# A new order at the start of a fused kernel: twelve units on half the tokens first, attention steps between products

## The chip, the cores and the metric

The kernel runs on one core of a Trainium2 chip. A core has a matrix engine (PE in the rows, with its weight loads on PEld), a vector engine (DVE), a scalar engine (ACT), a general-purpose engine (POOL) and a queue engine (SP) that here only starts DMAs. Each engine works through its own list in order, and engines wait for one another by semaphores. The metric is the device time of one execution in microseconds, as the median of several runs.

## The reference, cut to what matters

Inputs are a decaying linear attention over 4 sequences of 768 tokens (8 heads of 48), a dense mixture of four experts, and a two-layer network:

```python
# attention: state S (complex, 48x48 per head) decays by a_re + i a_im, magnitude capped at 0.999
S = a_t * S + outer(k_t, v_t);  y_t = q_t @ real(S)
# mixture, x is 3072 x 384, four experts with 1024 hidden columns each
p = probs / (probs.sum(-1) + 1e-9)
out += p[:, e] * (relu(x @ w1[e]) @ w2[e])
# second network, 2048 hidden columns
h = out @ w_in;  result = maximum(0.01 * h, h) @ w_out
```

## The kernel before, in words

**Tiling.** The 3072 tokens are 24 chunks of 128 (attention) and 6 groups of 512 (the two networks); a group is four chunks. The hidden columns are cut into units of 128: 32 for the experts, 16 for the second network. Per group and unit, `gemm_in` does nine matmuls into a PSUM tile `ph` (each product of fp32 numbers is split into three fp32r products: high x high, high x low, low x high), DVE makes `hp` from it, ACT its high part `hh`, DVE its low part `hl`, and `gemm_out` does nine matmuls into three accumulators. The loop over `order` at the end issues `gemm_in(s + 2)` ahead of `gemm_out(s)`, so a unit has two positions of time for `hp`, `hh` and `hl`.

**Attention.** A chunk has two generators. `elementwise(c)` has 18 steps on DVE, ACT and POOL and ends in `ft`, which `by_head` reorders by six small DMAs into `hd`. `products(c)` does the matmuls: transposes `pt` (copied to `kt`), scores `sc` (masked to `att`), `pm` (the state update `st`), `py`, and transposes `px`, of which `xh` and `xl` are the input of the units.

**Weights.** A unit's raw weights (384 KB) come by DMA into one of four `raw` tiles, are split into a high and a low part `wt` (768 KB, one of seven tiles, `WTS`) by ACT (L408) and POOL (L409), and are stored to the scratch `ws`; the later five groups load them from there. For the first units, `cast_early` (letter `s`) and `rest_early` (letter `m`: two fp32 matmuls, L429 and L430, and an ACT copy) make the low part on the matrix engine.

**What sets the order.** Nothing is scheduled by a tool: engines run what the code issues, in the order of issue. Before the first unit the string `PLAN` sets it, a letter a step: `0` to `3` a step of `elementwise` of that chunk, `p` and `q` of `products(0)` and `(1)`, `s` and `m` as above, `n` the probabilities. Then the loop over `order` runs, and its `tick` (two per position, at most three steps each) takes steps from `background`: the rest of chunks 2 and 3, their products (`r`, `t`), then the chunks of the later groups, by the table `pace`. In the loop `split_unit(s + 4, 0)` and `split_unit(s + 3, 1)` are issued ahead of the ticks and of `split_h(s + 2)`, so on ACT a weight cast stands ahead of the `kt` copies and the `hh` of its position. `load_unit(s + 7)` is issued at the top of a position.

**The start.** The first 8 units (`NHALF`) of group 0 run on 256 tokens (chunks 0 and 1) while chunks 2 and 3 are still to come, then the same 8 units on the other 256 tokens, with their weights loaded again from `ws`, and then units 8 to 31 on 512 tokens. A "half block" below is nine matmuls of 256 columns, the `gemm_in` or the `gemm_out` of a unit on 256 tokens.

Of the kernel before, what the change touches and what calls it, by code (L numbers as in the profile page):

```python
# [10 lines left out]
F32 = mybir.dt.float32  # L11
# [20 lines left out]
WU = 2 * DM  # L32
AR_MIN = 0.76
NHALF = 8
PLAN = (
    "0101001010101011" "01ss0000mm" "00sss11mm000" "1111ppsm23111qq"
    "23232n3pp23p2ppqq3q23qqpq23m"
)
MAXT = 3
KN = 3.0  # L40
PT = 32
TPOOL = 6
MARGIN = 2.0
LAG = 2
E2 = 20
RAWS = 4
WTS = 7
DEC = 33.0
# [1 line left out]
ESTEPS = 17  # L50
LOADSTEP = 9
NSTEPS = ESTEPS + len(PSTEPS)
WAIT = 4
AR_MAX = 1e4
AI_MAX = 1.0
PI = 3.1415925
# [5 lines left out]
def fused_kernel(  # L62
# [13 lines left out]
    V, A, G, SP, PE = nc.vector, nc.scalar, nc.gpsimd, nc.sync, nc.tensor  # L76
# [6 lines left out]
    with ExitStack() as fast:  # L83
# [58 lines left out]
        def load_chunk(c, part=None):  # L142
            if part in (None, 0):
                pool = p_el2 if c in (1, 3) else p_in
                t = pool.tile([P, 4, NG, P], F32, name="aaqk", bufs=2)
                vt = pool.tile([P, DM], F32, name="vt", bufs=2 if c in (1, 3) else 3)
                inputs[c] = (t, vt)
            t, vt = inputs[c]
            if part is None:
                SP.dma_start(t, attn[c])  # L150
            else:
                SP.dma_start(t[:, 2 * part : 2 * part + 2], attn[c][:, 2 * part : 2 * part + 2])
            if part in (None, 1):
                SP.dma_start(vt, v[c])
# [3 lines left out]
        def table(name):  # L158
            if tables[0] != name:
                A.preload_act_table_set(name)  # L160
                tables[0] = name

        def elementwise(c):
            t, vt = inputs[c]
# [78 lines left out]
        def by_head(c):  # L243

            ft, vt = feats[c]
            pool = p_el2 if c in (1, 3) else p_el
            hd = pool.tile([2 * D, H, 2 * P + 1], F32, name="hd")
            for ri in range(2):
                for i in range(NG):
                    row = ri * D + i * DG  # L250
                    (A if c < 2 and (i == ri or i == 2 - ri) else SP).dma_start(hd[row : row + DG], ft[:, ri, i])
            feats[c] = (ft, hd, vt)


# [3 lines left out]
        def products(c):  # L258
# [7 lines left out]
            for ri in range(2):  # L266
                pt = ps_a.tile([P, NG, P], F32, name="pt", tag="pa")
                for i in range(NG):
                    PE.transpose(pt[:, i], ft[:, ri, i, P : 2 * P], ident)  # L269
                A.copy(  # L270
                    kt[:, :, ri * D : (ri + 1) * D].rearrange("t h (r d) -> t r d h", d=DG),
                    pt.rearrange("t r (d h) -> t r d h", h=H),
                )
                yield
# [25 lines left out]
            for h in range(H):  # L300
                PE.matmul(py[:, h], att[:, h], vt[:, h * D : (h + 1) * D], start=True, stop=first)  # L301
                if not first:
                    PE.matmul(py[:, h], hd[:, h, :P], old[:, h], start=False, stop=True)  # L303
                if h == 3:
                    yield
            y = pool.tile([P, DM], F32, name="y", bufs=1)
# [59 lines left out]
        whole, halves = (0, TG), ((0, TG // 2), (TG // 2, TG))  # L366
        first_stage = lambda g: [(g, u, whole) for u in range(NU1)]
        second_stage = lambda g: [(g, u, whole) for u in range(NU1, NU)]
        order = [(0, u, half) for half in halves for u in range(NHALF)] + first_stage(0)[NHALF:]
        begins = [0]  # L370
        for g in range(1, NGRP):
            begins.append(len(order) - NHALF)
# [6 lines left out]


        raws, wts, pbs, hs, x2 = {}, {}, {}, {}, {}
        seen = set()
        fresh = [u not in seen and not seen.add(u) and u < NU1 for _, u, _ in order]

        def load_unit(s):

# [7 lines left out]
        def load_split(s):  # L394
            if s >= len(order):
                return
            u = order[s][1]
            if not fresh[s]:
                wts[s] = p_w.tile([P, 2, 2, DM], F32R, name="wt", bufs=WTS)
                SP.dma_start(wts[s].bitcast(F32), ws[u])  # L400

# [34 lines left out]
        def load_pb(s):  # L436
            if s >= len(order) or order[s][1] >= NU1 or order[s][1] % 8 or order[s][2][0]:
                return
            g, e = order[s][0], order[s][1] // 8
            pb = p_h.tile([P, TG], F32, name="pb", bufs=2)  # L440
            SP.dma_start(pb, pn_d[e : e + 1, g * TG : (g + 1) * TG].to_broadcast([P, TG]))
            pbs[g, e] = pb

# [32 lines left out]
        def gemm_out(s, acc):  # L476
            u, (t0, t1) = order[s][1:]
            first, last = u in (0, NU1) and t0 == 0, u in ends
            wt = wts.pop(s)[:, 1]
            hh, hl = hs.pop(s)  # L480
            for dc in range(NG):
                cols = slice(dc * P, (dc + 1) * P)
                out = acc[dc][:, t0:t1]
                PE.matmul(out, wt[:, 0, cols], hh, start=first, stop=False)  # L484
                PE.matmul(out, wt[:, 1, cols], hh, start=False, stop=False)  # L485
                PE.matmul(out, wt[:, 0, cols], hl, start=False, stop=last)  # L486


        def zipped(*gens):
            gens = list(gens)  # L490
            while gens:
                for x in list(gens):
                    if next(x, gens) is gens:
                        gens.remove(x)
                yield

        def run_all(*gens):
            gens = list(gens)
            while gens:
                gens = [x for x in gens if next(x, gens) is not gens]  # L500

        with tc.manual_schedule():
            table("natural_log_exp_and_others")
# [9 lines left out]
                load_unit(s)  # L513
            steps = {str(c): elementwise(c) for c in range(CPG)}
            steps.update(zip("pqrt", (products(c) for c in range(CPG))))
            early_halves = iter([(s, part) for s in range(6) for part in (0, 1)][: PLAN.count("s")])
            for x in PLAN + "m" * 8:
# [9 lines left out]
            for s in (5, 6):  # L527
                load_unit(s)
            split_unit(3, 0)

            def background():
                for _ in range(2):
                    next(steps["2"])
                    yield
                for _ in zipped(steps["2"], steps["3"]):
                    yield
                load_chunk(4)
                for _ in range(WAIT):
                    yield
                for x in "rt":  # L540
                    yield from steps[x]
# [29 lines left out]

            dec = decoding()

            first = 2 + max(0, ESTEPS + 1 - min(PLAN.count("2"), PLAN.count("3"))) + WAIT + E2 - PLAN.count("r") - PLAN.count("t")
# [34 lines left out]
            for s in range(len(order)):  # L609
# [12 lines left out]
                if u not in ends:  # L622
                    tick(now)
                split_h(s + 2, hp)
                if fresh[s]:
                    SP.dma_start(ws[u], wts[s].bitcast(F32))
                gemm_out(s, acc)
                now += step
# [214 lines left out]
```

## Time and profile before

| | |
|---|---|
| median of 3 runs | 1481.2 us (1477.52 to 1483.52) |
| profiled execution | 1478.36 us, span 1476.6 us |
| PE busy | 1402.4 us, 95% of the span |
| DVE, ACT, POOL busy | 59%, 38%, 18% |
| mean granted clock of PE | 0.976 |
| first unit's first matmul | 66.74 us |
| first half block on tokens 256 to 511 | 123.46 us |
| group 0's accumulators read out | 285.67 us |

The span is the time from the first to the last instruction of the profiled execution; 1.76 us of that execution lie around it. PE is busy nearly all the time from 170 us on, so what stands between a shorter time and this one is either matmul work or the idle and slow stretches of the first 170 us. A granted clock of 1.00 is 2.4 GHz, 0.50 is 1.2 GHz. A row of the time line gives start, duration, engine, line, operation and tile, with the idle time before it and what ended it in brackets; an fp32 matmul shows as two records, and a record's duration overlaps the next one's start.

### The profile page before, as it was taken

To read this page: it belongs to the slowest core of one execution; us is meant where nothing else is said; L and a number is where in the kernel's file an instruction comes from. 1 tells how busy PE (TensorE), PEld (TensorE's weight loads), DVE (VectorE), ACT (ScalarE), POOL (GpSimd) and SP (SyncE) were. 2 spreads that over 40 slices of the span, in tenths; PEclk is the share of its full clock that TensorE was granted. 3 is DMA by queue.
4 is the path that set the end of the run, shared out by engine and by line. 5 is a ranking of instruction groups with operands and counts; after the bars stand their busy time and mean duration, and the time that the engine had idled before them with its cause. 6 is when DMAs were issued, how large, how long until landed. Compare 5 with 4: busy or idle time off the path is not lost.

```text
span 1476.6 us, 18540 instructions
## 1 busy us (share of the span) xinstructions
PE 1402.4 (95%) x6978; PEld 1177.2 (80%) x6978; DVE 864.7 (59%) x1504; ACT 564.8 (38%) x961; POOL 264.5 (18%) x244
## 2 busy tenths in 40 slices
PE   3858999999999999999999999999999999999997
PEld 1858888888777888788888888888888888888886
DVE  7556887788988898785454554554443333333332
ACT  5424565444345434455234354233332111323232
POOL 2120565412223223221011110110110000100000
PEclk9569999999999999999999999999999999999999
DMA  7288789986788789588567477576465665556561
GB/s 192 43 207 301 212 255 298 331 291 208 273 301 290 250 305 319 153 303 245 153 234 222 151 242 216 188 222 199 154 199 172 231 207 196 190 188 208 190 212 65
DMA packets 91043, 325.49 MB, mean 220 GB/s; under 512 B 10464, under 2 KB 32064, under 8 KB 90944
## 3 DMA queue, kind: packets, MB, share of 16 engines
q1 hardware_dynamic: 87488, 318.71, 67.1%
q10 hardware_dynamic: 3456, 5.51, 1.3%
q8 instruction: 56, 0.92, 0.3%
q14 instruction: 43, 0.35, 0.1%
HBM read 262.72 MB, written 42.52 MB: 207 GB/s over the span
## 4 chain that ended last, share of the span: by engine, by line
PE 58%; DVE 2%; ACT 0%; issue 0%; DVEq 0%; ACTq 0%
PE ph L455 27%; PE acc L484 9%; PE acc L486 9%; PE acc L485 9%; PE sc L280 1%; PE py L301 1%; PE py L303 1%; PE pm L289 1%; PE pt L269 0%; DVE hl L473 0%; DVE hp L460 0%; PE px L311 0%; DVE d L349 0%; ACT hh L472 0%; DVE d L355 0%
## 5 line engine op out<-in xcount | busy, mean ns | idle before, releaser
L455 PE MATMUL ph<-xh,wt 128*128 128x512 f32 (+1 forms) x1200 | 397.9, 388 | 0.0
L484 PE MATMUL acc<-hh,wt 128*128 128x512 f32 (+1 forms) x888 | 350.8, 395 | 5.2 <-ACT o L604 5.1
L486 PE MATMUL acc<-hl,wt 128*128 128x512 f32 (+1 forms) x888 | 342.9, 386 | 4.5 <-DVE hl L473 4.5
L485 PE MATMUL acc<-hh,wt 128*128 128x512 f32 (+1 forms) x888 | 341.5, 385 | 0.0
L472 ACT CAST hh<-hp 128x512 fp32r<-128x512 f32 (+1 forms) x296 | 180.4, 610 | 418.2 <-DVE hp L460 326.5
L473 DVE TENSOR_TENSOR hl<-hp,hh 128x512 fp32r<-128x512 f32 (+1 forms) x296 | 213.4, 721 | 150.3 <-ACT hh L472 149.1
L455 PEld LDWEIGHTS ph<-xh,wt 128*128 128x128 f32 x1200 | 225.5, 190 | 42.4 <-ACT ge L121 0.3
L460 DVE SCALAR_TENSOR_TENSOR hp<-ph,pb 128x512 f32<-128x512 f32 (+1 forms) x200 | 133.0, 665 | 189.9 <-PE ph L455 188.6
L455 PE MATMUL ph<-xl,wt 128*128 128x512 f32 (+1 forms) x600 | 230.2, 384 | 0.0
L486 PEld LDWEIGHTS acc<-hl,wt 128*128 128x128 f32 x888 | 167.3, 188 | 40.0 <-DVE hl L473 6.0
L455 PE MATMUL ph<-x2h,wt 128*128 128x512 f32 x576 | 198.3, 398 | 0.0
L484 PEld LDWEIGHTS acc<-hh,wt 128*128 128x128 f32 x888 | 167.7, 189 | 36.5 <-ACT o L604 5.8
L485 PEld LDWEIGHTS acc<-hh,wt 128*128 128x128 f32 x888 | 168.0, 189 | 30.7
L463 DVE SCALAR_TENSOR_TENSOR hp<-hp 128x512 f32<-128x512 f32 x96 | 72.0, 750 | 185.0 <-ACT hp L462 184.9
L455 PEld LDWEIGHTS ph<-xl,wt 128*128 128x128 f32 x600 | 114.1, 190 | 20.3 <-DVE xl L320 0.2
L455 PEld LDWEIGHTS ph<-x2h,wt 128*128 128x128 f32 x576 | 108.7, 189 | 25.1
L462 ACT COPY hp<-ph 128x512 f32<-128x512 f32 x96 | 56.3, 586 | 178.5 <-PE ph L455 178.5
L455 PE MATMUL ph<-x2l,wt 128*128 128x512 f32 x288 | 114.5, 397 | 0.0
L409 POOL TENSOR_TENSOR wt<-raw,wt 128x384 fp32r<-128x384 f32 x58 | 65.0, 1142 | 62.4 <-ACT wt L408 62.3
L643 POOL TENSOR_TENSOR x2l<-o,x2h 128x512 fp32r<-128x512 f32 x18 | 25.2, 1424 | 256.4 <-ACT x2h L642 256.4
L301 PE MATMUL py<-vt,att 128*128 128x48 f32 x384 | 70.9, 280 | 0.1
L280 PEld LDWEIGHTS sc<-hd 96*128 96x128 f32 x384 | 54.2, 208 | 15.4 <-issue 7.9
(97 smaller groups left out, 1482.2 us busy)
## 6 DMA issues: line engine op xcount, KB each, us to landing
wt<-ws_scratch SPq DMA_DIRECT2D x264, 768.0 KB, 4.8
ws_scratch<-wt SPq DMA_DIRECT2D x32, 768.0 KB, 7.5
hd<-ft SPq DMA_DIRECT2D x138, 128.5 KB, 5.4
aaqk<-in_attn_dram SPq DMA_DIRECT2D x22, 768.0 KB, 8.9
raw<-in_w_dram SPq DMA_DIRECT2D x32, 384.0 KB, 4.5
r<-in_w_dram SPq DMA_DIRECT2D x32, 384.0 KB, 7.4
ws_scratch<-dw SPq DMA_DIRECT2D x32, 384.0 KB, 6.2
pb<-pn_scratch SPq DMA_DIRECT2D x24, 256.0 KB, 6.5
```

The costliest lines, as they stand in the source:

```text
L280: PE.matmul(sc[:, j], hd[:, h, P : 2 * P], hd[:, h, :P], start=True, stop=True)
L301: PE.matmul(py[:, h], att[:, h], vt[:, h * D : (h + 1) * D], start=True, stop=first)
L409: G.tensor_tensor(wt[:, 1], raw, wt[:, 0].bitcast(F32), ALU.subtract)
L455: PE.matmul(ph[:, : t1 - t0], wt[:, wi, cols], x[kc][:, t0:t1], start=n == 0, stop=n == 3 * NG - 1)
L460: V.scalar_tensor_tensor(hp, ph, 0.0, pbs[g, u // 8][:, t0:t1], ALU.max, ALU.mult)
L462: A.copy(hp, ph)
L463: V.scalar_tensor_tensor(hp, hp, 0.01, hp, ALU.mult, ALU.max)
L472: A.copy(hh, hp)
L473: V.tensor_tensor(hl, hp, hh.bitcast(F32), ALU.subtract)
L484: PE.matmul(out, wt[:, 0, cols], hh, start=first, stop=False)
L485: PE.matmul(out, wt[:, 1, cols], hh, start=False, stop=False)
L486: PE.matmul(out, wt[:, 0, cols], hl, start=False, stop=last)
```

## The change

- `NHALF` is 12: twelve units run first on tokens 0 to 255. Units 6 to 11 then go on with tokens 256 to 511 on the `wt` tiles that they still hold (`kept`). Units 12 to 25 follow on 512 tokens. Units 0 to 5 come back for tokens 256 to 511, one ahead of each of units 26 to 31, with their raw weights loaded and split a second time. A unit is stored to `ws` when its second half (or its whole) runs.
- `PLAN` has twelve `s` and twelve `m` for six, so six units are made ready on PE instead of three; they stand between the products of chunks 0 and 1. Chunk 1's `kt` copies go from ACT to DVE, three of its `hd` DMAs from ACT's queue to SP's, and `warm` adds four fp32 matmuls of 384 columns to `products(1)`, whose output nobody reads.
- The steps left of chunks 2 and 3 come in the order of `LATER`, mostly chunk 2 first, and 22 empty steps (`WAIT`) stand ahead of their products, with chunk 4's load after the 14th.
- The row of probabilities of experts 0 and 1 for group 0 gets tiles that last.

```diff
-NHALF = 8
+NHALF = 12
+AGAIN = 6
 PLAN = (
-    "0101001010101011" "01ss0000mm" "00sss11mm000" "1111ppsm23111qq"
-    "23232n3pp23p2ppqq3q23qqpq23m"
+    "0101001010101011" "01ss0000mm" "00sss11mm000" "1111ppsmsm23111L"
+    "23n22qqsmsm33ppsm22p3ppmsqqm3qsm2233qqpqm"
 )
+LATER = "23222232232223333333"
-KN = 3.0
+KN = 5.0
-E2 = 20
+E2 = 17
-WAIT = 4
+WAIT = 22
+LOAD4 = 14
...
+        def warm(n):
+            out = ps_acc.tile([P, TG], F32, name="warm", tag="acc0")
+            for _ in range(n):
+                PE.matmul(
+                    out[:, : NG * P], ident, inputs[0][0][:, 0].rearrange("p g t -> p (g t)"),
+                    start=True, stop=True,
+                )
...
-                    (A if c < 2 and (i == ri or i == 2 - ri) else SP).dma_start(hd[row : row + DG], ft[:, ri, i])
+                    (A if c == 0 and (i == ri or i == 2 - ri) else SP).dma_start(hd[row : row + DG], ft[:, ri, i])
...
-                A.copy(
+                (V.tensor_copy if c == 1 else A.copy)(
...
+                if c == 1 and h % 2:
+                    warm(1)
...
-        order = [(0, u, half) for half in halves for u in range(NHALF)] + first_stage(0)[NHALF:]
+        order = [(0, u, halves[0]) for u in range(NHALF)]
+        order += [(0, u, halves[1]) for u in range(AGAIN, NHALF)]
+        order += first_stage(0)[NHALF : NU1 - AGAIN]
+        for u in range(AGAIN):
+            order += [(0, u, halves[1]), (0, NU1 - AGAIN + u, whole)]
+        kept = {NHALF + i: AGAIN + i for i in range(NHALF - AGAIN)}
...
-        fresh = [u not in seen and not seen.add(u) and u < NU1 for _, u, _ in order]
+        fresh = [g == 0 and u < NU1 and s not in kept for s, (g, u, _) in enumerate(order)]
...
-            if not fresh[s]:
+            if s in kept:
+                wts[s] = wts[kept[s]]
+            elif not fresh[s]:
...
-                for _ in range(2):
-                    next(steps["2"])
+                for x in LATER:
+                    next(steps[x], None)
                     yield
-                for _ in zipped(steps["2"], steps["3"]):
-                    yield
-                load_chunk(4)
-                for _ in range(WAIT):
+                for k in range(WAIT):
+                    if k == LOAD4:
+                        load_chunk(CPG)
                     yield
...
-                if fresh[s]:
+                if g == 0 and u < NU1 and t1 == TG:
                     SP.dma_start(ws[u], wts[s].bitcast(F32))
```

On PE, from the transposes of chunk 1 to the second score product, the program before has (`raw`/`ident` with `wt`/`minus` is one `m`):

```order
L269 MATMUL pt<-ident,ft 128x128 x6
L280 MATMUL sc<-hd 128x128 x8
L289 MATMUL pm<-vt,kt 96x48 x8
L301 MATMUL py<-vt,att 128x48 x8
L280 MATMUL sc<-hd 128x128 x8
```

and the changed one (buffer numbers tell the tiles of units 3 and 4 apart):

```order
L281 MATMUL pt_341<-ident_96,ft_161 128x128 x3
L281 MATMUL pt_346<-ident_96,ft_161 128x128 x3
L449 MATMUL ph_352<-raw_143,ident_96 128x384
L450 MATMUL ph_352<-wt_283,minus_106 128x384
L449 MATMUL ph_358<-raw_143,ident_96 128x384
L450 MATMUL ph_358<-wt_283,minus_106 128x384
L292 MATMUL sc_366<-hd_252 128x128 x4
L292 MATMUL sc_372<-hd_252 128x128 x4
L449 MATMUL ph_379<-raw_145,ident_96 128x384
L450 MATMUL ph_379<-wt_356,minus_106 128x384
L301 MATMUL pm_390<-vt_119,kt_267 96x48 x8
L313 MATMUL py_404<-vt_119,att_365 128x48 x8
```

Three `m` now stand ahead of `pm` of chunk 0; three more follow between `py` of chunk 0 and `py` of chunk 1, and the four `warm` matmuls inside the latter. Before, one `m` stood after all of this.

On SP, from the row of probabilities on, the queue before has (`hd_606` and `hd_615` are chunks 2 and 3):

```order
L441 DMA pb_340<-pn_scratch 128x512
L392 DMA raw_467<-in_w_dram 128x768
L392 DMA raw_469<-in_w_dram 128x768
L392 DMA raw_509<-in_w_dram 128x768
L626 DMA ws_scratch<-wt_206 128x1536
L626 DMA ws_scratch<-wt_231 128x1536
L251 DMA hd_606<-ft_288 16x8x257 x6
L251 DMA hd_615<-ft_297 16x8x257 x6
```

and the changed one (`hd_645` and `hd_694` are chunks 2 and 3, `raw_674` and `raw_714` units 10 and 11):

```order
L464 DMA pb0_335<-pn_scratch 128x512
L410 DMA raw_547<-in_w_dram 128x768
L410 DMA raw_588<-in_w_dram 128x768
L410 DMA raw_626<-in_w_dram 128x768
L464 DMA pb1_628<-pn_scratch 128x512
L263 DMA hd_645<-ft_294 16x8x257 x6
L410 DMA raw_674<-in_w_dram 128x768
L263 DMA hd_694<-ft_303 16x8x257 x6
L410 DMA raw_714<-in_w_dram 128x768
```

The stores have left this stretch, and the raw weights of units 10 and 11 stand behind the reordering of chunks 2 and 3.

On PE the products of chunk 2 now begin after the `gemm_in` of ten units (it was five) and those of chunk 3 after eight `gemm_out`; between the first score product of chunk 2 and the first half block on tokens 256 to 511 stand five half blocks, as before.

## Rows read from the trace of the kernel before

**Rows 1.** Windows: busy us (instructions) of PE, PEld, DVE, ACT, POOL; clock, DMA share, GB/s.
```profile
37.00:66.74 29.74, 25.53 (x123) 24.03 (x121) 14.12 (x34) 10.58 (x20) 0.00 (x0) 0.50 0.21 39
...
71.66:90.40 18.74, 7.94 (x50) 7.24 (x49) 18.46 (x31) 7.01 (x14) 8.70 (x8) 0.73 0.40 127
...
95.70:123.46 27.76, 26.05 (x185) 25.57 (x186) 7.41 (x14) 4.37 (x10) 1.00 (x1) 0.78 1.01 346
123.46:170.00 46.54, 40.98 (x267) 36.61 (x265) 37.28 (x73) 27.12 (x49) 17.59 (x16) 0.96 0.72 214
200.00:260.00 60.00, 58.77 (x316) 49.57 (x316) 47.71 (x74) 36.44 (x66) 37.80 (x34) 1.00 0.89 270
```

**Rows 2.** Waits of PE in the first 260 us: total, times, longest.
```profile
PE pt L269 <- DVE ft L234: 14.7, 4, 9.4
```

**Rows 3.** Time line of PE up to the first unit.
```profile
19.47 1.49 PE L429 MATMUL ph<-raw,ident 128*128 128x384 f32 x2
20.75 1.49 PE L430 MATMUL ph<-wt,minus 128*128 128x384 f32 x2
...
24.97 0.81 PE L429 MATMUL ph<-raw,ident 128*128 128x384 f32 x2
25.62 0.81 PE L430 MATMUL ph<-wt,minus 128*128 128x384 f32 x2
...
32.91 1.51 PE L269 MATMUL pt<-ident,ft 128*128 128x128 f32 x6 [3.76 <-DVE ft L234]
36.47 3.79 PE L280 MATMUL sc<-hd 96*128 96x128 f32 x16 [2.04 <-ACT kt L270]
44.47 2.79 PE L289 MATMUL pm<-vt,kt 128*96 128x48 f32 x16 [4.21 <-DVE att L281]
...
56.50 0.63 PE L301 MATMUL py<-vt,att 128*128 128x48 f32 x2
...
63.33 1.67 PE L311 MATMUL px<-ident,y 128*128 128x128 f32 x6
```

**Rows 4.** Time line of PE after the first unit, the same kinds at 2.4 GHz.
```profile
71.35 0.28 PE L455 MATMUL ph<-xh,wt 128*128 128x256 f32 x1
...
72.43 0.28 PE L484 MATMUL acc<-hh,wt 128*128 128x256 f32 x1
...
112.35 1.16 PE L280 MATMUL sc<-hd 96*128 96x128 f32 x8 [0.56 <-ACT kt L270]
...
115.32 1.48 PE L289 MATMUL pm<-vt,kt 128*96 128x48 f32 x16
...
122.01 0.55 PE L311 MATMUL px<-ident,y 128*128 128x128 f32 x3 [0.57 <-ACT y L307]
```

**Rows 5.** Issues of SP: the reordering of chunks 2 and 3.
```profile
86.75 7.71 SPq L251 DMA_DIRECT2D hd<-ft  x12
```

**Rows 6.** DMA from 60 to 140 us: issues, size of one, median us to landing.
```profile
raw<-in_w_dram SPq DMA_DIRECT2D x6, 384.0 KB, 5.8
```

**Rows 7.** Time line of ACT beside chunk 2's transposes.
```profile
91.14 1.47 ACT L270 COPY kt<-pt 128x384 f32<-128x384 f32 x2
92.41 0.93 ACT L408 CAST wt<-raw 128x384 fp32r<-128x384 f32 x2
```

**Rows 8.** Chain that ended last: one of its pieces, a block of 512 columns.
```profile
1459.11 2.10 PE ph L455 x9
```

**Rows 9.** Time line of DVE: an operation beside POOL's work, and alone.
```profile
71.66 1.22 DVE L210 SCALAR_TENSOR_TENSOR tb<-ge 128x384 f32<-128x384 f32 x1
...
77.51 0.55 DVE L210 SCALAR_TENSOR_TENSOR tb<-ge 128x384 f32<-128x384 f32 x1
...
86.64 1.22 DVE L473 TENSOR_TENSOR hl<-hp,hh 128x256 fp32r<-128x256 f32 x1
...
91.26 0.42 DVE L473 TENSOR_TENSOR hl<-hp,hh 128x256 fp32r<-128x256 f32 x1 [0.53 <-ACT hh L472]
```

**Rows 10.** POOL's weight splits, 200 to 260 us, by the view of windows for their line.
```profile
200.00:260.00 60.00, 24.92 (x23) 1.00 0.89 270
```

More of the change, by code (lines that the diff above doesn't have):

```diff
@@ L145, in load_chunk @@
                 t = pool.tile([P, 4, NG, P], F32, name="aaqk", bufs=2)
-                vt = pool.tile([P, DM], F32, name="vt", bufs=2 if c in (1, 3) else 3)
+                vt = (p_el2 if c == 1 else p_in).tile([P, DM], F32, name="vt", bufs=1 if c == 1 else 3)
                 inputs[c] = (t, vt)
@@ L381, in fused_kernel @@
         raws, wts, pbs, hs, x2 = {}, {}, {}, {}, {}
-        seen = set()
-        fresh = [u not in seen and not seen.add(u) and u < NU1 for _, u, _ in order]
+        fresh = [g == 0 and u < NU1 and s not in kept for s, (g, u, _) in enumerate(order)]
         def load_unit(s):
@@ L439, in load_pb @@
             g, e = order[s][0], order[s][1] // 8
-            pb = p_h.tile([P, TG], F32, name="pb", bufs=2)
+            if g == 0 and e * 8 < NHALF:
+                pb = pools["raw"].tile([P, TG], F32, name=f"pb{e}")
+            else:
+                pb = p_h.tile([P, TG], F32, name="pb", bufs=2)
             SP.dma_start(pb, pn_d[e : e + 1, g * TG : (g + 1) * TG].to_broadcast([P, TG]))
@@ L478, in gemm_out @@
             first, last = u in (0, NU1) and t0 == 0, u in ends
-            wt = wts.pop(s)[:, 1]
+            wt = wts[s][:, 1]
             hh, hl = hs.pop(s)
@@ L486, in gemm_out @@
                 PE.matmul(out, wt[:, 0, cols], hl, start=False, stop=last)
[L489 to L494, printed above, removed]
-                yield
[L497 to L500, printed above, removed]
         with tc.manual_schedule():
@@ L515, in fused_kernel @@
             steps.update(zip("pqrt", (products(c) for c in range(CPG))))
-            early_halves = iter([(s, part) for s in range(6) for part in (0, 1)][: PLAN.count("s")])
-            for x in PLAN + "m" * 8:
+            early_halves = iter([(s, part) for s in range(7) for part in (0, 1)][: PLAN.count("s")])
+            for x in PLAN:
                 if x in steps:
@@ L526, in fused_kernel @@
                     rest_early()
-            for s in (5, 6):
-                load_unit(s)
-            split_unit(3, 0)
+                elif x == "L":
+                    load_unit(5)
+                    load_unit(6)
             def background():
-                for _ in range(2):
-                    next(steps["2"])
+                for x in LATER:
+                    next(steps[x], None)
                     yield
-                for _ in zipped(steps["2"], steps["3"]):
-                    yield
-                load_chunk(4)
-                for _ in range(WAIT):
+                for k in range(WAIT):
+                    if k == LOAD4:
+                        load_chunk(CPG)
                     yield
@@ L572, in fused_kernel @@
             dec = decoding()
-            first = 2 + max(0, ESTEPS + 1 - min(PLAN.count("2"), PLAN.count("3"))) + WAIT + E2 - PLAN.count("r") - PLAN.count("t")
+            first = len(LATER) + WAIT + E2
             pace = [(0.0, 0), (KN, first)]
```

## Prediction

> **What bounds the kernel now.** I read the busy shares by stretch first. From 200 to 260 us PE is busy for 58.77 of 60 us at a clock of 1.00 [rows 1]: the body is matmul work, which the change hardly touches. The loss is at the start, in three places. From 37.00 to 66.74 PE has work for 25.53 of 29.74 us, but at a clock of 0.50. From 71.66 to 90.40 DVE is busy for 18.46 of 18.74 us and PE for 7.94: the steps of chunks 2 and 3 are the bound there [rows 1], and the list of what PE waited for shows its longest such wait, 9.4 us, at transposes that need an `ft` [rows 2]. From 95.70 to 123.46 the products of chunks 2 and 3 run with a mean clock of 0.78. After that, to 170 us, PE lacks 5.56 us (46.54 less 40.98) [rows 1].
>
> **The first unit's start.** The program before reaches it at 66.74. From chunk 1's transposes at 32.91 I add up PE's new queue. The transposes take 1.5 at 1.2 GHz, and the first `m` two matmuls of 1.28 from start to start, 2.56 [rows 3]. These matmuls are dense; in the old trace a row of them from 18 us on went from 1.28 each to 0.65 each by 24.97 [rows 3], so I take 2.4 GHz behind the first one. The other five `m` then take 1.30 each, 6.5. The two score products take 2.2 each (16 records; 8 take 1.16, with some overlap), `pm` 1.5 each, `px` 1.0 for both chunks [rows 4]. `py` of chunk 1 took 6.83 at half clock (56.50 to 63.33, [rows 3]), so some 3.6 at full, and that of chunk 0, with half as many matmuls, 1.8. Four `warm` of 0.65 make 2.6. Then 0.6 for the copy of `y` (the wait at 122.01, [rows 4]) and 1.7 from the end of `px` to the first unit, as before (63.33 plus 1.67, to 66.74). Together 1.5 + 2.6 + 6.5 + 4.4 + 3.0 + 5.4 + 2.6 + 0.6 + 1.0 + 1.7 = 29.3, and with 0.3 for small waits on ACT's copies the first unit is at **62.5**. The old waits of 2.04 and 4.21 [rows 3] are filled by this work. The bounds are 60.5, if the clock is up a step earlier and no copy is late, and 79, which is a rival below. Chunk 1's `kt` copies on DVE come ahead of the scores by the time of an `m`; they cost nothing unless one lasts over 1.5 us. Three more `hd` on SP are 1.9 us of issue (7.71 for twelve, [rows 5]), with over 10 us to go until chunk 1's scores need them.
>
> **From there to the second half of the tokens.** DVE's work up to chunk 3's `ft` is the 18.74 us of rows 1, with three more small operations of 0.42 for the extra units and without the slow `hl` of 1.22 [rows 9], so about 19.2. It starts 4.1 us behind the first unit (4.9 before: the scans at L203 now come earlier). Chunk 3's `ft` is done 23.3 us behind the first unit, at 85.8; bounds are 20.5, if no operation meets POOL's work, and 28, if all six `hp` and `hl` take 1.22. Meanwhile PE has ten `gemm_in` and seven `gemm_out` of 1.08 us (71.35 to 72.43, [rows 4]), 18.4 us, and waits for DVE's `hl` for some 9 us in all: unit 5's `hl` stands right behind that `ft`, then come three half blocks and chunk 2's transposes, done at about 91.
>
> Then a new wait comes. SP has the raw weights of unit 11 behind chunk 3's six reorderings: half of 7.71, 3.9 us of issue [rows 5], then 5.8 us to landing [rows 6], so 95.5. On ACT the cast of unit 11 stands ahead of chunk 2's `kt` copies, so behind the waiting cast are queued these copies and the next `hh`, and PE's scores of chunk 2 wait for the first copy. Two casts, 0.93, and a copy, 0.8 [rows 7], give 97.2 for the scores, which before began at 95.70 [rows 1]. From there the mix is the old one, products of both chunks and five half blocks, 27.76 us. A mean clock of 0.78 over them [rows 1] is 6.1 us of full-speed work lost; behind a shorter idle stretch I give back 2.5 of it, and charge 1.0 because the first half block on the second tokens now stands right behind `px` and must wait for `xh` and `xl`. That makes 26.3, and **123.5** for that half block, against 123.46.
>
> The times are equal, but there the program before has done 14 half blocks and the changed one 22. Eight half blocks of 1.08 are **8.6 us** of work that fitted into time when PE waited for DVE.
>
> **The rest.** (a) Eight pairs of half blocks, 2.16, replace blocks of 2.10 [rows 8]: 0.5 more. (b) To 170 us the old program loses 5.56 us, partly while eight reloads of 768 KB share the DMA; now six units keep their tiles. Between nothing and all of it I take 1.5 off, nearer to nothing because DVE's steps of chunk 4 stay. (c) In the last six pairs units 0 to 5 are split a second time, 12 splits on POOL and 12 casts on ACT. POOL makes 23 splits in 60 us [rows 10], two a unit, so a unit takes 5.2 us and six pairs, nine units' work, 47 us. POOL then has 24 splits of 1.08, 26 us, and of other work (37.80 less 24.92 in 60 us) 10, so 36 of 47. DVE has 47.71/60 of 47 [rows 1], 37.4. Beside POOL's work an operation of DVE took 0.67 more (1.22 against 0.55), another 0.80 more [rows 9]; twelve times 0.80 is 9.6, and 37.4 + 9.6 = 47.0, so the cover is just used up. Most operations are not caught so; I charge 1.0, with bounds of 0 and 3.4 (all 13.0 us of the twelve splits added to DVE's 37.4). The DMA there has per pair two raw loads of 384 KB and two stores of 768 KB, 2.36 MB in 7.8 us, 302 GB/s and with the chunks' loads about 350, which rows 1 show moved (346) over 27.76 us.
>
> The Trainium skill ("GPSIMD Engine Reference", section 8, "Key points") says that GpSimd shares its SBUF interfaces with VectorE and contends with VectorE's instructions in a two-port mode or with two SBUF inputs. The trace agrees: `hl`, which has two such inputs, took 1.22 and 0.42 us [rows 9]. By that rule taken to its end the bound of 3.4 us would hold in (c), and the third rival below is that case; by the rows alone it is 1.0.
>
> **Sum.** 8.6 - 0.5 + 1.5 - 1.0 = 8.6 us off the profiled execution's 1478.36 (its span of 1476.6 and 1.76 around it) is 1469.8. That execution stands 2.8 below the median, 1481.2, from which it would be 1472.6. Forecast **1471**, between the two.
>
> **Rivals.** *The clock stays low at the start* (slower than before). If it stays at 0.50 up to the first unit, as it did from 37.00 to 66.74 although PE was busy for 25.53 us [rows 1], five more `m` behind 32.91 cost 12.8 and four `warm` 5.1, less 6.3 for the filled waits, and half a microsecond for the sixth ahead of it: the first unit is at 79, 16.3 later than forecast, and all that follows too: 1487. It decides from a first unit at 71.1, where the 8.6 us are gone. For it: sixteen score records in a row did not lift the clock in the old trace. Against it: the `m` did, between 20.75 and 24.97 [rows 3]. Chance 0.10. *The new wait does not come*: unit 11's weights land before ACT reaches its cast, and the clock holds over the products. Chunk 2's scores then start right behind its transposes, 5 us earlier, and 3 us more of the clock's loss come back: 1463. For it: half of SP's work ahead, chunk 2's reorderings, is long through by then. Against it: the rest stands in order. Chance 0.18. *The gain is given back later*: DVE is the bound in the last six pairs, 3.4 us for the 1.0, and over the second halves, where it has the same steps for less PE time, so that the 1.5 of (b) turns into a loss of as much: 1476. For it: rows 9 and the 5.56 us. Against it: 37.4 of 47. Chance 0.17. That the twelve units only move work, and fill no idle time, is excluded by PE's 7.94 of 18.74 us, unless the first unit is late.
>
> **How the numbers follow.** The forecast has 0.55, with a range of its own of 1464 to 1477. About 0.5%, 7.4 us, is what a measurement of this kernel can tell from no change: faster is below 1473.8, slower above 1488.6. Faster: 0.40 of the forecast's share, the second rival's 0.18, a little of the third: 0.60. Slower: part of the first, and whatever I have missed: 0.07. Same: 0.33. The range leaves out half of the first rival and of the second's far side: 1458 to 1483.
>
> **What would show it.** The first unit near 62.5, with a clock of 1.00 from about 40 us on. Waits of PE for `hl` of some 9 us until 86. ACT idle ahead of a weight cast, released by a raw load, and behind it chunk 2's `kt` copies; PE's scores of chunk 2 near 97. The first half block on the second tokens near 123.5. PE all but full in the last six pairs, with POOL at some 0.77. A first unit behind 68, or scores of chunk 2 behind 102, would make the forecast wrong on the slow side; scores at 92 on the fast one.

## The result: slower, and the profile after

The changed kernel takes 1490.75 us (median of 4 runs, 1489.54 to 1495.55), the kernel before 1481.32 (1477.52 to 1483.52): a ratio of 1.0069, 95% interval 1.0049 to 1.0089. The forecast was 1471 us, with a range of 1458 to 1483. The profiled execution of the changed kernel took 1495.55 us with a span of 1493.8; it is the slowest of the four, 4.8 above their median, so its sums are read with that in mind. The profiled run of the kernel before lies on the other side, 3.0 below its median.

**Up to 124 us the times came as forecast.** PE's time line of the kernel after, from the first unit to the first half block on the second tokens (start, duration, engine, line, operation; in brackets the wait and its releaser):

```profile
61.30 0.39 PE L478 MATMUL ph<-xh,wt 128*128 128x256 f32 x1 [0.62 <-ACT xh L333]
...
89.89 0.82 PE L281 MATMUL pt<-ident,ft 128*128 128x128 f32 x6
98.31 1.65 PE L292 MATMUL sc<-hd 96*128 96x128 f32 x6 [7.60 <-ACT kt L282]
...
124.23 0.39 PE L478 MATMUL ph<-xh,wt 128*128 128x256 f32 x1 [0.57 <-ACT xh L333]
```

The first unit stands at 61.30 (forecast 62.5, before 66.74), chunk 2's transposes at 89.89 (91), its scores at 98.31 (97.2), the half block at 124.23 (123.5). ACT's time line shows the new wait where it was put, a cast held by raw weights, with the `kt` copies behind it [rows 6, 7]:

```profile
96.61 0.92 ACT L428 CAST wt<-raw 128x384 fp32r<-128x384 f32 x2 [6.56 <-DMA raw<-in_w_dram]
97.44 1.48 ACT L282 COPY kt<-pt 128x384 f32<-128x384 f32 x2
```

With 22 half blocks done in place of 14 the kernel is ahead by 8 x 1.08 less 0.77 later, 7.9 us. Against a median run of the kernel before the lead is likely larger: run 9 below, the same program up to there, took 31.00 us at a clock of 0.68 for the products of chunks 2 and 3, where the profiled run took 27.76 at 0.78, and was 3.3 us later at its eighth `hp`.

**Then the lead is lost.** I take the times of the `hp` operations from DVE's time line, count them in half blocks (an `hp` of 512 columns counts as two), and compare equal counts. The changed kernel is ahead of the kernel before by 10.1 us at the 16th, 8.0 at the 28th, 3.2 at the 32nd, -2.3 at the 44th, -9.2 at the 52nd, -14.7 at the 64th. The 64th, before and after:

```profile
275.43 0.69 DVE L460 SCALAR_TENSOR_TENSOR hp<-ph,pb 128x512 f32<-128x512 f32 x1 [0.15 <-PE ph L455]
```

```profile
290.13 0.69 DVE L483 SCALAR_TENSOR_TENSOR hp<-ph,pb 128x512 f32<-128x512 f32 x1 [1.00 <-PE ph L478]
```

Group 0's read-out starts at 299.0 and not at 285.7. The windows view shows the stretch from the 13th `hp` to that read-out, after and then before (columns as in [rows 1]):

```profile
126.00:299.00 173.00, 156.10 (x865) 136.05 (x864) 124.70 (x209) 89.99 (x166) 82.53 (x75) 0.91 0.78 238
```

```profile
139.80:285.70 145.90, 140.61 (x773) 119.80 (x773) 115.11 (x180) 83.23 (x151) 78.51 (x70) 0.99 0.86 264
```

The stretch is 27.1 us longer. PE is idle for 16.9 in place of 5.3 us of it; the other 15.5 is PE being busy longer, mostly at the low clock: 9% of 173.0 against 1% of 145.9 is a difference of some 14 us of full-speed work (the two clocks are rounded to hundredths). What PE waited for there, after (total, times, longest):

```profile
PE sc L292 <- DMA hd<-ft: 9.7, 2, 7.0
PE pm L301 <- DVE att L293: 3.2, 1, 3.2
PE sc L292 <- ACT wt L428: 2.2, 1, 2.2
PE ph L478 <- POOL wt L429: 1.6, 1, 1.6
```

and before, in its stretch:

```profile
PE pm L289 <- DVE att L281: 2.0, 1, 2.0
PE sc L280 <- DMA hd<-ft: 1.5, 2, 1.1
```

The clock is low behind the three longest of these waits, on PE's time line of the kernel after:

```profile
164.86 2.05 PE L292 MATMUL sc<-hd 96*128 96x128 f32 x8 [7.03 <-DMA hd<-ft]
...
199.50 2.05 PE L292 MATMUL sc<-hd 96*128 96x128 f32 x8 [2.24 <-ACT wt L428]
...
240.02 2.64 PE L301 MATMUL pm<-vt,kt 128*96 128x48 f32 x16 [3.17 <-DVE att L293]
```

Ahead of each wait it was 1.00 (windows of 155.00 to 157.80, 194.00 to 197.20 and 234.00 to 236.80). The windows behind them (the first takes in part of the wait):

```profile
162.00:169.00 7.00, 4.14 (x15) 3.70 (x16) 5.43 (x11) 4.04 (x7) 3.68 (x3) 0.53 1.05 385
199.50:206.00 6.50, 6.50 (x21) 5.63 (x22) 3.40 (x6) 3.56 (x6) 5.17 (x5) 0.50 1.02 410
240.00:251.00 11.00, 10.98 (x50) 10.40 (x51) 9.61 (x16) 3.35 (x8) 6.49 (x6) 0.53 0.67 222
```

The third is the dearest: 11 us nearly all at 1.2 GHz behind a wait of 3.17. The Trainium skill ("TensorE: Matmul & The Clock Gate", section "HAM oscillation — how this bites in real kernels") describes this for waits on a DMA between pieces of matmul work: the array falls to its low rate and the work behind each wait runs cold. The trace agrees for the first wait, which was on a DMA, with a clock of 0.50 from 164.86 to 167.00. The other two were on ScalarE and VectorE, with the same clock behind them, and a wait of 2.49 us in the kernel before did not bring the clock down (last section).

Why the features of chunk 4 were late is seen in SP's own queue, after:

```profile
115.06 0.73 SPq L635 DMA_DIRECT2D ws_scratch<-wt  x1
143.19 0.33 SPq L410 DMA_DIRECT2D raw<-in_w_dram  x1
...
150.72 0.33 SPq L410 DMA_DIRECT2D raw<-in_w_dram  x1
...
153.23 0.33 SPq L410 DMA_DIRECT2D raw<-in_w_dram  x1
153.67 4.66 SPq L263 DMA_DIRECT2D hd<-ft  x6
```

From 115.8 to 143.2 the queue stands at one load of raw weights, whose buffer is freed by a split that POOL makes only then; two more such loads stand ahead of the `hd` reorderings of chunk 4. The last steps of its `ft` on DVE, and the reorderings, after and then before:

```profile
147.17 2.65 DVE L246 TENSOR_TENSOR ft<-cs,aaqk 128x768 f32<-128x768 f32 x2
```

```profile
142.64 1.78 DVE L234 TENSOR_TENSOR ft<-cs,aaqk 128x768 f32<-128x768 f32 x1
144.45 4.61 SPq L251 DMA_DIRECT2D hd<-ft  x6
```

The reorderings leave at 153.67 in place of 144.45. Of these 9.2 us the queue is 3.9, from the end of `ft` at 149.82; the other 5.4 is DVE, whose `ft` was done at 144.42 before. POOL makes the splits that the six kept tiles had postponed at one go, beside DVE's steps of chunk 4 (POOL, and three scans of DVE, after; then the same scans before, where POOL was at work for the first 0.8 us of them):

```profile
139.89 3.27 POOL L429 TENSOR_TENSOR wt<-raw,wt 128x384 fp32r<-128x384 f32 x3
147.19 6.01 POOL L429 TENSOR_TENSOR wt<-raw,wt 128x384 fp32r<-128x384 f32 x4 [4.03 <-ACT wt L428]
```

```profile
139.11 3.25 DVE L228 TENSOR_TENSOR_SCAN th<-ones,th,tr 128x128 f32<-128x128 f32 x3
```

```profile
135.64 1.87 DVE L216 TENSOR_TENSOR_SCAN th<-ones,th,tr 128x128 f32<-128x128 f32 x3
```

**And 3.9 us go after group 0**, where the two kernels do the same work: from the read-out to the end 1194.8 us against 1190.9 (windows of group 1 and of all the rest, after, then before):

```profile
299.00:471.50 172.50, 165.75 (x867) 138.87 (x866) 148.87 (x268) 77.07 (x129) 45.32 (x40) 1.00 0.79 266
299.00:1493.80 1194.80, 1172.11 (x5680) 976.49 (x5679) 668.59 (x1150) 426.18 (x709) 162.87 (x139) 1.00 0.67 219
```

```profile
285.70:456.70 171.00, 164.91 (x864) 138.57 (x863) 146.22 (x266) 77.03 (x129) 42.02 (x40) 1.00 0.79 264
285.70:1476.60 1190.90, 1170.60 (x5677) 975.88 (x5676) 662.93 (x1148) 424.45 (x707) 158.71 (x138) 1.00 0.67 219
```

The sum for the profiled runs: -7.9 at 124 us, +21.2 to the end of group 0, +3.9 after it, 17.2. For the medians, 9.4 apart, that leaves about 13.4 inside group 0, if the lead and the end are as in the two profiles.

### The profile page after: what moved, and what is told of

It is laid out like the page before. It is cut to its first block, busy times and chain, and to the rows that moved or that the text cites. A ratio compares the mean times of both kernels' runs of the same rounds, so it can differ in the third digit from the quotient of the medians.

```text
span 1493.8 us, 18779 instructions
## 1 busy us (share of the span) xinstructions
PE 1415.5 (95%) x7082; PEld 1186.0 (79%) x7082; DVE 870.5 (58%) x1514; ACT 572.2 (38%) x981; POOL 273.4 (18%) x250
## 4 chain that ended last, share of the span: by engine, by line
PE 57%; issue 0%; ACT 0%; DVE 0%
PE ph L478 26%; PE acc L507 9%; PE acc L509 9%; PE acc L508 9%; PE sc L292 1%; PE py L313 1%; PE py L315 1%; PE pm L301 1%; PE pt L281 0%; PE px L325 0%; DVE hp L486 0%; ACT o L613 0%; ACT hh L495 0%; ACT hp L485 0%; ACT dw L371 0%
## 5 line engine op out<-in xcount | busy, mean ns | idle before, releaser
L478 PE MATMUL ph<-xh,wt 128*128 128x512 f32 (+1 forms) x1224 | 402.3, 386 | 3.4 <-POOL wt L429 2.3
L507 PE MATMUL acc<-hh,wt 128*128 128x512 f32 (+1 forms) x900 | 354.7, 394 | 8.3 <-ACT o L613 5.0
L509 PE MATMUL acc<-hl,wt 128*128 128x512 f32 (+1 forms) x900 | 347.6, 386 | 1.7 <-DVE hl L496 1.6
L508 PE MATMUL acc<-hh,wt 128*128 128x512 f32 (+1 forms) x900 | 346.5, 385 | 0.0
L496 DVE TENSOR_TENSOR hl<-hp,hh 128x512 fp32r<-128x512 f32 (+1 forms) x300 | 218.5, 728 | 161.5 <-ACT hh L495 159.0
L478 PEld LDWEIGHTS ph<-xh,wt 128*128 128x128 f32 x1224 | 230.2, 191 | 46.4 <-POOL wt L429 3.2
L478 PE MATMUL ph<-xl,wt 128*128 128x512 f32 (+1 forms) x612 | 233.2, 381 | 0.6 <-DVE xl L334 0.5
L507 PEld LDWEIGHTS acc<-hh,wt 128*128 128x128 f32 x900 | 172.3, 191 | 40.3 <-ACT o L613 5.4
L509 PEld LDWEIGHTS acc<-hl,wt 128*128 128x128 f32 x900 | 172.0, 191 | 37.6 <-DVE hl L496 4.0
L508 PEld LDWEIGHTS acc<-hh,wt 128*128 128x128 f32 x900 | 172.7, 192 | 30.9
L429 POOL TENSOR_TENSOR wt<-raw,wt 128x384 fp32r<-128x384 f32 x64 | 72.5, 1154 | 51.6 <-ACT wt L428 44.3
L292 PE MATMUL sc<-hd 96*128 96x128 f32 x384 | 57.6, 301 | 19.5 <-DMA hd<-ft 9.7
L292 PEld LDWEIGHTS sc<-hd 96*128 96x128 f32 x384 | 56.1, 215 | 24.8 <-issue 10.5
```

The source lines that it names most:

```text
L292: PE.matmul(sc[:, j], hd[:, h, P : 2 * P], hd[:, h, :P], start=True, stop=True)
L429: G.tensor_tensor(wt[:, 1], raw, wt[:, 0].bitcast(F32), ALU.subtract)
L478: PE.matmul(ph[:, : t1 - t0], wt[:, wi, cols], x[kc][:, t0:t1], start=n == 0, stop=n == 3 * NG - 1)
L496: V.tensor_tensor(hl, hp, hh.bitcast(F32), ALU.subtract)
```

## Experiments

Each was timed over five rounds beside the kernel before, four kernels at a time on one chip; ratios are to it, with 95% intervals. The changed kernel stands at 1.0069. Each edit is to the changed kernel, if nothing else is said.

**1 to 4: is it the last six pairs, or the waits?** Spread:

```
-        order += first_stage(0)[NHALF : NU1 - AGAIN]
-        for u in range(AGAIN):
-            order += [(0, u, halves[1]), (0, NU1 - AGAIN + u, whole)]
+        for k, x in enumerate(first_stage(0)[NHALF:]):
+            order += [(0, k // 3, halves[1])] if k % 3 == 2 else []
+            order += [x]
```

> The six returning half blocks stand one behind each third unit of units 12 to 31, in place of one ahead of each of the last six; nothing else differs, and the work is the same. Theory A (the loss is made in the last six pairs, where every pair brings two loads of raw weights and two stores of tiles, 2.36 MB in about 6.5 us, and two splits): 1475 to 1482 us, and the lead over the kernel before at the end of group 0 is near 0 or above. Theory B (the loss comes from short waits of TensorE, for the re-laid features of chunks 4 to 7 and for splits, and from the clock at 0.50 behind each, wherever the halves stand): 1488 to 1492 us.

Measured: 1486.69 us, 1.0027 (1.0014 to 1.0039). Early store:

```
-                if g == 0 and u < NU1 and t1 == TG:
+                if g == 0 and u < NU1 and (t0 == 0 if u < AGAIN else t1 == TG):
```

> The tiles of units 0 to 5 are stored to DRAM at their first half block instead of at their second; order, loads and splits stay. It takes 0.79 MB out of each of the last six pairs. Theory A in its form 'the DMA is what is short there': 1480 to 1486 us. If it is the splits on ScalarE and GpSimd, or the waits of theory B: 1489 to 1492 us.

Measured: 1492.72 us, 1.0070 (1.0052 to 1.0088). Reload, on top of it (the line of the early store is left out here):

```
-        fresh = [g == 0 and u < NU1 and s not in kept for s, (g, u, _) in enumerate(order)]
+        fresh = [g == 0 and u < NU1 and s not in kept and (u >= AGAIN or not t[0]) for s, (g, u, t) in enumerate(order)]
```

> As the run before, and the returning half blocks read their stored tile back (0.79 MB each) instead of loading raw weights (0.39 MB) and splitting them again: 12 casts of ScalarE and 12 subtractions of GpSimd less in the last six pairs, 0.39 MB more per pair than the run before. If the second splits (GpSimd beside VectorE) are what costs: 1478 to 1485 us and below the run before. If the DMA is: 3 to 6 us above the run before. Theory B: 1488 to 1492 us.

Measured: 1486.63 us, 1.0028 (1.0016 to 1.0041). Eight halves (the six constants are put on one line here):

```
-NHALF, AGAIN, MAXT, KN, WAIT, LOAD4 = 12, 6, 3, 5.0, 22, 14
+NHALF, AGAIN, MAXT, KN, WAIT, LOAD4 = 8, 2, 4, 3.0, 10, 6
-        order += first_stage(0)[NHALF : NU1 - AGAIN]
+        order += first_stage(0)[NHALF : NU1 - 6]
         for u in range(AGAIN):
-            order += [(0, u, halves[1]), (0, NU1 - AGAIN + u, whole)]
+            order += [(0, u, halves[1]), (0, NU1 - 6 + u, whole)]
+        order += first_stage(0)[NU1 - 4 :]
```

> Eight first halves instead of twelve, six of which go on with their tiles, two come back (ahead of units 26 and 27); start, clock, casts and the order of chunks 2 and 3 as in the changed kernel. TensorE then waits for the second tokens again with 14 half blocks done (8.6 us of lead gone), and four of the six pairs are gone. Theory A: 1478 to 1483 us (about the kernel before). Theory B: the lead goes and the waits stay: 1493 to 1500 us.

Measured: 1484.13 us, 1.0008 (0.9994 to 1.0023). The early store does not settle whether the stores' bytes cost: it also delays the start (the 13th `hp` comes at 129.91 in place of 126.07), and the stretch from there to the read-out is shorter (166.0 us in place of 173.0). Spreading the halves gives 6 us on the changed kernel, and leaving out their second splits 6 us on the early store, each between the two theories' numbers, and eight halves do nearly as well as the kernel before although they give the lead up. By these four I held the crowded pairs for half of the cause. That did not last (below). In all four the stretch after group 0 took 1194.6 to 1195.8 us, so what is lost there is lost for another reason.

**5 and 9: the background's three steps.** The change rewrites the formula that counts the background's steps up to chunk 4 (`first`), and sets `E2` from 20 to 17. The old formula gave 36 where 33 steps exist, the new one gives 59 of 59.

```
-                pace.append((begins[g] - MARGIN, first + ESTEPS + (NSTEPS + 1) * CPG * g))
+                pace.append((begins[g] - MARGIN, first + 3 + ESTEPS + (NSTEPS + 1) * CPG * g))
```

> Only the due times of the background from group 1 on are raised by three steps; order, start and group 0's products of chunks 2 and 3 stay. The kernel before counted 36 steps up to its first group's chunk 4 where it had 33, so its background ran three steps ahead of its table in all later groups; the changed kernel counts 59 where it has 59. With the three steps given back, TensorE's instructions from group 1 on stand in the order of the kernel before. If the 3.9 us that the changed kernel loses after group 0 come from this shift: 1486 to 1488 us, and the stretch from the end of group 0 to the end takes about 1191 us instead of 1194.8. If they come from something else (places in memory, chip): 1490 to 1492 us.

Measured: 1482.34 us, 1.0010 (1.0002 to 1.0019). From the last product of group 0 on, PE's matmuls stand in the order of the kernel before again, and after group 0 it takes:

```profile
291.80:1482.40 1190.60, 1170.55 (x5678) 975.86 (x5676) 662.91 (x1148) 424.62 (x707) 158.95 (x138) 1.00 0.67 220
```

DVE is back to 662.91 us busy from 668.59 and POOL to 158.95 from 162.87: this fits two engines that meet more often with the shifted steps, but is not shown. And the ratio falls by 0.0059, 8.7 us (5.4 to 12.0 by the two intervals), twice what is lost after group 0 and better than the 1486 to 1488 us expected: the rest, some 4.5, comes inside it. The reverse, `first - 3` in the same line of the kernel before:

> The kernel before, with the due times of its background from group 1 on lowered by three steps, which gives it the steps of the changed kernel there; nothing of the start, of the order of half blocks or of group 0's first units is touched. If the place of the background among the units is the cause: 1485 to 1487 us, of it 3.9 us after the end of group 0. If not: 1481 to 1482 us.

Measured: 1482.05 us, 1.0005 (0.9994 to 1.0016). The stretch after group 0 took what was expected:

```profile
286.00:1481.00 1195.00, 1172.08 (x5680) 976.63 (x5679) 668.66 (x1150) 426.22 (x709) 162.49 (x139) 1.00 0.66 219
```

and yet the whole is only 0.7 us slower (-0.9 to 2.4), a miss: there the same shift gained some 3 us inside group 0.

**6, 13 and 16: SP's queue.** Raw weights six units ahead in place of seven, so that no load waits for a split not yet given out:

```
-                load_unit(s + 7)
+                if s != 15:
+                    load_unit(s + (7 if s < 15 else 6))
```

> From the sixteenth half block on raw weights are asked for six units ahead instead of seven, so that SyncE's queue waits for no split that has not been given out yet, and the pieces of chunk 4's features leave as soon as they are made (149.8 us) instead of at 153.7 us. If that queue wait is what gives the lead back in the middle: the wait for them falls from 7.0 to about 3 us, and 1485 to 1488 us. If the burst of splits beside VectorE does it, or the clock: 1489 to 1492 us.

Measured: 1487.53 us, 1.0043 (1.0028 to 1.0057), with 4.2 us of waits for `hd` in place of 9.7. SP's queue in this run:

```profile
142.11 0.34 SPq L410 DMA_DIRECT2D raw<-in_w_dram  x1
...
149.64 0.33 SPq L410 DMA_DIRECT2D raw<-in_w_dram  x1
150.08 3.80 SPq L263 DMA_DIRECT2D hd<-ft  x6
```

The long stop, up to 142.11, is still there. What has gone is one of the two loads between it and the reorderings. Together with the three steps:

> The three steps, and raw weights asked for six units ahead; the returning halves stay in the last six pairs. If the queue ahead of the features is what costs in group 0: their wait falls from 8.5 to about 3 us, and 1477 to 1480 us, as with the spread. If the crowded pairs cost beside it: 1482 to 1484 us.

Measured: 1478.99 us, 0.9986 (0.9974 to 0.9999). What PE waited for from 124.5 us to the end of group 0 in this run, and the window of that stretch:

```profile
PE pt L281 <- DVE ft L246: 3.0, 2, 1.6
PE px L325 <- ACT y L321: 2.2, 3, 1.9
PE ph L478 <- POOL wt L429: 1.8, 1, 1.8
PE sc L292 <- ACT wt L428: 1.6, 1, 1.6
PE sc L292 <- DMA hd<-ft: 1.6, 1, 1.6
```

```profile
123.60:283.10 159.50, 146.30 (x867) 125.94 (x866) 133.49 (x211) 90.44 (x168) 87.64 (x76) 0.99 0.79 251
```

The clock is 0.99 again, and 13.5 us of the 173.0 are gone (this profiled run is 2.0 below its median, and the other 4.8 above its own). The view of SP's waits shows the long stop in both, 27.3 and 27.5 us, and tells them apart by the reorderings' own wait; first the changed kernel, then this run:

```profile
SPq L410 <- POOL wt L429: 108.1, 21, 27.3
...
SPq L263 <- DVE ft L246: 3.6, 2, 3.2
```

```profile
SPq L410 <- POOL wt L429: 84.3, 16, 27.5
...
SPq L263 <- DVE ft L246: 13.7, 3, 7.9
```

In the changed kernel the features wait for the queue; here the queue waits for the features, and chunk 4's leave at 148.15. Another way to the same, from order index 22 on (with the three steps and the six units):

```
-                SP.dma_start(raws[s].rearrange("p a b -> p (a b)"), w[u])
+                (G if s > 21 else SP).dma_start(raws[s].rearrange("p a b -> p (a b)"), w[u])
```

> The three steps, raw weights six units ahead, and from order index 22 on they are asked for from GpSimd's queue, so that SyncE's queue holds none of them. If the queue ahead of the features is the cost: the wait for them falls to what the transfer itself needs, 1476 to 1480 us. If issuing from GpSimd costs VectorE or the splits: 1481 us or more.

Measured: 1481.53 us, 1.0004 (0.9995 to 1.0014). The waits for `hd` were 2.5 us, but POOL was busy for 93.22 and DVE for 139.03 us in that stretch: its time is in the second range expected, and it gives away what it gains.

**14 and 15: more time for the same transfers.** The scores two steps later, with the three steps, and with the six units as well:

```
-PSTEPS = (1, 3, 5, 12, 14, 17, 20, 22, 24)
+PSTEPS = (1, 3, 5, 14, 16, 18, 20, 22, 24)
```

> The three steps, and in the table of the background the two steps of the scores of a chunk stand two places later (at 14 and 16 in place of 12 and 14, the one behind at 18), about 1.8 us more between the features' transfers and the scores that need them. The queue is not touched. If TensorE's wait for the transfers is what costs: their wait falls by 1.5 to 2 us per chunk that waits, and 1477 to 1481 us. If the wait is only another face of a late VectorE or of crowded splits: 1481 to 1484 us.

Measured: 1508.05 us, 1.0182 (1.0168 to 1.0196).

> Both of the runs before. If the wait for the features is the cost: no such wait above 1.5 us is left, the clock from the thirteenth half block to the end of group 0 is 0.98 or more, and 1473 to 1478 us. If other waits take its place (products waiting for ScalarE and VectorE): 1478 to 1482 us.

Measured: 1507.43 us, 1.0182 (1.0167 to 1.0196). These are the worst misses. Some 11 us of the loss against run 5 come inside group 0 and 12 after it (1202.8 and 1202.4 us for 1190.6). PE's waits in group 0 of the second:

```profile
PE pm L301 <- DVE att L293: 15.6, 3, 7.5
PE py L313 <- DVE att L293: 3.6, 1, 3.6
```

No wait for `hd` is left, and it is worse: the masks of the scores (`att`) now stand too close ahead of the products that need them, behind DVE's other steps, and the clock of the stretch is 0.90. So it is not the transfers as such: a wait of PE for another engine can cost as much, with the clock behind it.

**7, 8 and 10 to 12: do the gains add?** Spread, store, reload and the three steps; then with the first unit behind the kept tiles (order index 18) split at the twelfth half block, and the next at the fifteenth (a line that marks a split as made is left out here):

```
+                if s in (11, 14):
+                    for k in range(18, 19 if s == 11 else 20):
+                        split_unit(k, 0)
+                        split_unit(k, 1)
                 split_unit(s + 4, 0)
```

> The spread of the returning halves, the early store and reload of their tiles, and the three steps together. If the second splits cost because they are crowded into the last six pairs, the first two remove the same cost and don't add: 6 us and 4 us off, 1480 to 1482 us. If they cost wherever they stand, they add: 1475 to 1479 us. The kernel before lies near 1482.

> As the run before, and the first unit after the six kept tiles (order index 18) is split at the twelfth half block, while GpSimd idles, and the next at the fifteenth. In the changed kernel seven half splits came at one go at 139.9 to 153.2 us, beside VectorE's work on chunk 4, where VectorE's scans took 1.08 us each in place of about 0.35. If this burst gives back the lead: 3 to 6 us below the run before. If the late features do, whatever the splits: the same within 1.5 us.

Measured: 1478.86 us, 0.9989 (0.9978 to 0.9999), and 1478.30, 0.9985 (0.9976 to 0.9993). Spread and steps without store and reload, then with the six units, then with the early split:

> The spread returning halves and the three steps, without the early store and the reload. The early store held the queue in the first half blocks, so that the thirteenth came at 131 us in place of 124.5 us in the run with both. If the crowding of second splits is all that the spread removes: 1475 to 1478 us, below the run with store and reload. If the three steps had already taken the pairs' loss away: 1481 to 1483 us, as with the three steps alone.

> As the run before, with raw weights asked for six units ahead. Alone this gained 3.9 us on the changed kernel, in the middle of group 0 (a lead of 7.3 us at the fortieth half block, where the changed kernel had 2.4). If the queue wait is a cost of its own: 3 to 4 us below the run before, 1471 to 1475 us. If it is eaten up later in group 0: within 1.5 us of the run before.

> As the run before, with the first unit after the kept tiles split at the twelfth half block and the next at the fifteenth. If the burst of splits still costs once the queue is free: 1 to 3 us below the run before. If not: within 1 us of it.

Measured: 1487.18 us, 1.0041 (1.0023 to 1.0059); 1479.26, 0.9990 (0.9981 to 0.9999); 1478.67, 0.9984 (0.9975 to 0.9993). The spread gains 6 us on the changed kernel, loses 4.6 with the three steps, and does nothing (0.0004) with the steps and the free queue. In its bad run, which no range expected, PE waited 10.5 us for `hd`, longest 7.3, and the free queue brought that to 2.9 and the time down by 7.6 us, where 3 to 4 were expected. The early split, which moves two of the postponed splits to 128 us, gives nothing that can be told.

So two causes add up, each undone alone and both together: the three steps (0.0059, with an interval of 0.0022 to either side), the queue (0.0026, 0.0025 to either side), both 0.0083. The queue's part is near the noise when it is undone alone; it is clear with the three steps (1.0010 to 0.9986) and with steps and spread (1.0041 to 0.9990). Neither the spread nor the early split adds to these two; the early store and the reload were not run beside the freed queue.

## Why the prediction was wrong

- *The first unit, the second tokens, the new wait of ACT*: right, each within 1.3 us. On the way there two errors cancel: PE was idle for 5.8 us from 61.30 to 86.00, with 4.9 of waits for `hh` and `hl`, where 9 for `hl` were forecast, and the clock of 0.87 there, where none was charged, is another 3.2. The first two rivals, a clock that stays low and a wait that doesn't come, are both refuted by the rows above.
- *The 8.6 us of lead*: right in place and size (7.9).
- *The step that failed is "The rest"*, in two places. Its term (b) let the stretch to 170 us gain 1.5, because the kept tiles need no reload. What the kept tiles also do was not worked out: no raw buffer comes free while they run, SP stops for 27.3 us, two loads behind the stop wait for splits that come in a burst, and chunk 4's features leave 9.2 us later than before (3.9 by the queue, 5.4 by DVE), just where the lead brings PE there sooner: the waits for `hd` grow from 1.5 to 9.7 us. Taking one load out of that queue is worth 3.9 us (0.2 to 7.5), and 3.6 (1.4 to 5.8) with the steps. I counted only SP's issues ahead of unit 11 [rows 5] and never asked what the queue waits for afterwards.
- *"The body ..., which the change hardly touches"* is the other place. The diff sets `E2` and rewrites `first`; I did not count the steps of both versions, which would have shown 36 for 33 against 59 for 59 and a background three steps later in every later group: 3.9 us after group 0 and, in this kernel, some 4.5 inside it. Between the forecast and the measurement lie 19.8 us; undoing both causes takes back 12.3.
- *Term (c)*, 1.0 for the last six pairs, can't be judged alone. Much of the loss falls there by the clock on the wall, and spreading or reloading seemed to prove it, but with both causes undone the place of the halves makes no difference. The sign named for these pairs, PE all but full and POOL at 0.77, did not come: from 225 to 290 us PE was at 0.91 and POOL at 0.56. DVE, at 0.72, had time left, and was not the bound by its total as the third rival had it; but PE's dearest wait there, up to 240.02, was for DVE's mask `att`:

```profile
225.00:290.00 65.00, 59.17 (x346) 53.04 (x345) 46.80 (x76) 34.03 (x66) 36.38 (x34) 0.89 0.91 282
```

- *The third rival* ("given back later") had the right direction, with 5 us as its price; 17.3 were given back (7.9 of lead, 9.4 of loss), and none of my prices held the clock behind a wait.

Open: why the three steps cost some 4.5 us inside group 0 here but gain some 3 in the kernel before, why the spread changes its sign, and where the rest of the lead goes (the best version keeps 2 of 7.9 us). All of it lies in group 0. On the first, the waits give a hint and no proof: PE's wait for `att`, 3.2 us in the changed kernel, stands in runs 2 (3.1) and 6 (4.6) too, is 1.3 with the reload (3), and is gone with the spread (1) and with the three steps given back (5). On the rest, one difference was never run alone: with `KN` at 5.0 the table lays the 125 steps of chunks 4 to 7 over 25 units' time in place of 27, so DVE's steps come closer together in group 0.

## What to carry to other kernels

A lead won on one engine is kept only if all that feeds it comes sooner too: follow each in-order queue past the change and ask which buffer it waits for next and what stands behind that wait. Where a table or a counted offset sets when background work comes, count its real steps before and after; an offset of three moved work that the diff never names. Price a wait of TensorE with the low clock that can follow it, which here cost more than the waits.

## What was not expected of the hardware

- Waits of 2.24 to 3.17 us on ScalarE or VectorE were followed by 6.5 and 11 us at a granted clock of 0.50 and 0.53. The low clock cost more (some 14 us of full-speed work) than the additional idle time (11.6). Length alone does not decide: in the kernel before a wait of 2.49 us for `hl` was followed by a clock of 1.00 up to 146 us:

```profile
139.29 0.39 PE L486 MATMUL acc<-hl,wt 128*128 128x256 f32 x1 [2.49 <-DVE hl L473]
```

- From the end of group 0 to the end the programs took 1189.9 to 1192.1 us wherever the background stands as in the kernel before (that kernel and the runs with the three steps given back, other than the two with later scores), and 1194.4 to 1195.8 wherever it stands three steps later (the changed kernel, runs 1 to 4 and 6, and the kernel before with its steps taken off). These are sixteen profiles with different beginnings: three places in a table of 27 steps a chunk are worth 4 us, and the beginnings make no difference above 2.2 us there.
